# A decode kernel with a gated mix: small loads ahead of w_gate, and the block's end moved ahead of wo's rest

## The chip, the core and the metric

The kernel runs on one core of one Trainium2 chip. Its metric is device microseconds of one execution, as the median of the runs shown; smaller is better. All times below are microseconds unless marked otherwise. Engines are named as in the profile: PE (TensorE matmuls), PEld (its weight loads), DVE (VectorE), ACT (ScalarE), POOL (GpSimd) and SP (SyncE, which issues every load and store of this kernel).

## What is computed

One token of a decoder. Attention with 32 query heads over 8 key/value heads, a cache of 32768 positions and a head size of 128, mixed by a gate with a SwiGLU feed-forward layer. All inputs are bf16.

```python
x = A_x                                        # 1 x 1 x 512
g = sigmoid((x * gate_w).sum(-1, keepdims=True))
q = x @ wq                                     # 512 -> 32 heads x 128
p = softmax(q @ k_cache^T * 128 ** -0.5)       # per head, 4 heads share one of 8 k/v heads
a = (p @ v_cache) as one row of 4096, @ wo     # 4096 -> 512
b = (silu(x @ w_gate) * (x @ w_up)) @ w_down   # 512 -> 1792 -> 512
out = g * a + (1 - g) * b                      # 1 x 1 x 512
```

The caches hold 8 x 32768 x 128 values each, 67 MB for k and 67 MB for v; with the weights 148 MB are read and 1 KB is written.

## The kernel before, in words

The kernel is written engine by engine inside one block (`nc.Block("main")`, L212). Each engine has its own instruction list, and all order between engines is by semaphores written out by hand. Where the block ends, all five engines meet in a barrier: each drains and counts up a semaphore, POOL collects the counts and releases the others. The profile books these instructions on L212.

**SP** (L221 to L271) issues every transfer in one order. First wq (L248), x (L249), the gate's weights (L250), w_gate and w_up (L252, both counting up `sem_f`). Then, for each of the 8 k/v heads g, two halves of k of 4 MB each (`load_k`, L227) and v of 8 MB (`load_v`, L238; the last head's v in two halves, L244). A k load waits until PE has transposed what stood in its page, a v load until PE has used the v before it; the first v load waits until PE is done with w_gate and w_up, whose page it takes over. Behind the last v come w_down (L259) and wo in five pieces of 16, 8, 4, 2 and 2 rows of each partition (L265, `WO_CUTS`), each with a semaphore of its own. Then SP waits for the result row (`sem_dve_row`), stores it (L267) and waits for the store to land.

**PE.** `emit_start` (L385) makes the identity matrix, transposes x, computes q, the gate's sum and the feed-forward layer's first half, and then loops over the 8 heads: `emit_k` twice (transposes of k at L279, copied out by DVE at L646, and scores at L291), `emit_max`, `emit_v` (L332) and `emit_reduce` (L353). `emit_end` (L479) is what comes behind the loop: w_down's 14 strips, the head outputs brought into place, and wo piece by piece. Pieces 0 and 1 (24 rows) go through `emit_strip` (L364), four accumulating strips of 512; ACT copies these strips to SBUF (L543, counting up `sem_part`). Pieces 2 to 4 (8 rows) go through `emit_rows` (L375), four matmuls of 128 columns each; behind piece 2 four more such matmuls add ACT's copy. In the instruction list `emit_end` stands ahead of `emit_start`: a loop of two turns runs `emit_start` in the first turn and `emit_end` in the second.

**ACT** loops over the heads (exponentials, L530; copy of the accumulated outputs, L539), then waits for the last reduction and for PE's strips and makes the copy at L543. **DVE** ends with the transposed outputs (L696), the column vector `O2` (L698) and, when PE has summed everything, the result row (L700). **POOL** sets constants and passes on one semaphore.

Of the kernel before, what the change touches and what calls it, by code (L numbers as in the profile page):

```python
# [5 lines left out]
ACT = mybir.ActivationFunctionType  # L6
ALU = mybir.AluOpType
AX = mybir.AxisListType
BF16 = mybir.dt.bfloat16
# [3 lines left out]
def bass_gated_mix__gqa_block_cached__swiglu_ffn__decode_kernel(  # L13
# [14 lines left out]
    G = A_k_cache.shape[1]  # L28
# [23 lines left out]
    STEP = 16  # L52
    WOJ = H * DH // 128
# [3 lines left out]
    WO_CUTS = [0, 16, 24, 28, 30, 32]  # L57
    WO_ROWS = 24
    OC = NOUT // 128
# [3 lines left out]
    NSTRIP = 4  # L63
# [11 lines left out]
    with ExitStack() as es:  # L75
        def S_(name):
            return es.enter_context(nc.semaphore(name))
# [5 lines left out]
        sem_wo = [S_(f"s_wo{i}") for i in range(len(WO_CUTS) - 1)]  # L83
# [37 lines left out]
        sem_red = S_("s_red")  # L121
# [5 lines left out]
        sem_pe_part = S_("s_pe_part")  # L127
        sem_part = S_("s_part")
        sem_pe_sum = S_("s_pe_sum")
        sem_dve_row = S_("s_dve_row")  # L130
        sem_out = S_("s_out")

        def T(name, shape, dt):
            return es.enter_context(nc.sbuf_tensor(name, shape, dt))
# [11 lines left out]
        sel4 = T("sel4", [128, 16], FP32)  # L146
# [5 lines left out]
        tT = T("tT", [128, FC], BF16)  # L152
        wd = T("wd", [128, FC, NOUT], BF16)
# [15 lines left out]
        O2a = T("O2a", [128, WOJ], BF16)  # L169
        O2 = T("O2", [128, WOJ], BF16)  # L170
        res_row = T("res_row", [128, 128], BF16)

        def P(name, shape, dt):
            return es.enter_context(nc.psum_tensor(name, shape, dt))
# [15 lines left out]
        ps_c = ps_sc[0][:, :]  # L190
        ps_s = ps_sc[1][:, 0:HPG]
        ps_d = ps_sc[1][:, 0:128]
# [11 lines left out]
        part = acc[:, :, :].rearrange("p q d -> p (q d)")  # L204
# [4 lines left out]
        wo_v = page[:, PG_X, 0 : WOJ * NOUT].rearrange("p (j n) -> p j n", j=WOJ)  # L209
        qall = qblk[:, :].rearrange("p (g e c) -> p g e c", e=2, c=2 * HPG)  # L210

        with nc.Block("main") as block:  # L212
            @block.gpsimd
            def _(pool):
                pool.memset(ones_f[:, :], 1.0).then_inc(sem_ones, 1)
                pool.memset(ones_bf[:, :], 1.0).then_inc(sem_ones, 1)
                for g in range(G - 1):
                    pool.wait_ge(sem_v[0], 16 * (g + 1))
                    pool.sem_inc(sem_v[1], 16)

            @block.sync  # L221
            def _(sp):
                def load_k(g, b):
                    if g:
                        sp.wait_ge(sem_fill, UPG * (g - 1) + UPP * (b + 1))
                    src = A_k_cache[0, g, :, :].rearrange("(p b r) d -> p b r d", b=NB, r=R)
                    sp.dma_start(  # L227
                        page[:, PG_K[b], :].rearrange("p (r d) -> p r d", d=DH), src[:, b, :, :]
                    ).then_inc(sem_k[b], 16)

                def load_v(g):
                    if g:
                        sp.wait_ge(sem_v_free, STEP * g)
                    else:
                        sp.wait_ge(sem_pe_h, 1)
                    src = A_v_cache[0, g, :, :].rearrange("(p b r) d -> p b r d", b=NB, r=R)
                    if g < G - 1:
                        sp.dma_start(  # L238
                            vpage.rearrange("p b r d -> p (b r d)"),
                            src.rearrange("p b r d -> p (b r d)"),  # L240
                        ).then_inc(sem_v[0], 16)
                    else:
                        for b in range(NB):
                            sp.dma_start(vpage[:, b, :, :], src[:, b, :, :]).then_inc(  # L244
                                sem_v[b], 16
                            )

                sp.dma_start(wq_v, A_wq.rearrange("(p c) n -> p c n", c=KC)).then_inc(sem_q, 16)  # L248
                sp.dma_start(x_row[0:1, :], A_x[0, :, :]).then_inc(sem_ld_x, 16)  # L249
                sp.dma_start(gw_row[0:1, :], gate_w.unsqueeze(0)).then_inc(sem_ld_g, 16)  # L250
                for w, src in enumerate((B_w_gate, B_w_up)):
                    sp.dma_start(  # L252
                        wgu[:, w, :, :], src.rearrange("(p c) f -> p c f", c=KC)
                    ).then_inc(sem_f, 16)
                for g in range(G):
                    for b in range(NB):
                        load_k(g, b)
                    load_v(g)
                sp.dma_start(  # L259
                    wd[:, :, :], B_w_down.rearrange("(p j) n -> p j n", j=FC)  # L260
                ).then_inc(sem_ld_wd, 16)
                src = A_wo.rearrange("(p j) n -> p j n", j=WOJ)
                for k, s in enumerate(sem_wo):
                    a, b = WO_CUTS[k], WO_CUTS[k + 1]
                    sp.dma_start(wo_v[:, a:b, :], src[:, a:b, :]).then_inc(s, 16)  # L265
                sp.wait_ge(sem_dve_row, 1)
                sp.dma_start(  # L267
                    out[0, 0, :].rearrange("(c n) -> c n", c=OC),
                    res_row[0 : 32 * (OC - 1) + 1 : 32, :],
                ).then_inc(sem_out, 16)  # L270
                sp.wait_ge(sem_out, 16)  # L271

            @block.tensor
            def _(pe):
# [67 lines left out]
                def emit_reduce(i):  # L342
# [15 lines left out]
                            stop=(q == RQ - 1),  # L358
                        )
                    ins.then_inc(sem_red, STEP)  # L360

                def emit_strip(w, vec, j, start, stop):
                    c = j % NSTRIP
                    return pe.matmul(  # L364
                        ps_c[32 * c : 32 * c + 1, :],
                        vec[:, j : j + 1],
                        w[:, j, :],
                        start=start,
                        stop=stop,
                        skip_group_check=True,  # L370
                    )

                def emit_rows(lhsT, rhs, start, stop):
                    for oc in range(OC):
                        ins = pe.matmul(  # L375
                            ps_d[32 * oc : 32 * oc + 1, :],
                            lhsT,
                            rhs[:, oc * 128 : (oc + 1) * 128],
                            start=start,
                            stop=stop,  # L380
                            skip_group_check=True,
                        )
                    return ins

                def emit_start():  # L385
                    pe.wait_ge(sem_dve_r, 1)
# [92 lines left out]
                def emit_end():  # L479
                    pe.wait_ge(sem_dve_tT, 1)  # L480
                    pe.wait_ge(sem_ld_wd, 16)
                    for j in range(FC):
                        emit_strip(wd, tT, j, j < NSTRIP, False)

                    pe.wait_ge(sem_dve_oT2, 1)
                    pe.matmul(
                        ps_m[:, M_O0 : M_O0 + WOJ], pmat[:, :], O2a[:, :], start=True, stop=True
                    ).then_inc(sem_pe_O2, 1)
                    pe.wait_ge(sem_dve_O2, 1)
                    for k, s in enumerate(sem_wo):  # L490
                        pe.wait_ge(s, 16)
                        for j in range(WO_CUTS[k], WO_CUTS[k + 1]):
                            if j < WO_ROWS:
                                ins = emit_strip(wo_v, O2, j, False, j >= WO_ROWS - NSTRIP)
                            else:
                                ins = emit_rows(
                                    O2[:, j : j + 1], wo_v[:, j, :], j == WO_ROWS, j == WOJ - 1
                                )
                        if WO_CUTS[k + 1] == WO_ROWS:
                            ins.then_inc(sem_pe_part, 1)  # L500
                        if WO_CUTS[k] == WO_ROWS:
                            pe.wait_ge(sem_part, 1)
                            emit_rows(sel4[:, 0:1], part, False, False)
                    ins.then_inc(sem_pe_sum, 1)

                with pe.Fori(0, 2, 1) as turn:
                    with pe.If(turn > 0):
# [5 lines left out]
            def _(act):  # L513
# [7 lines left out]
                with act.Fori(0, G * STEP, STEP) as i:  # L521
# [15 lines left out]
                            ).then_inc(sem_exp, 2)  # L537
                    act.wait_ge(sem_v_free, i + STEP)
                    act.activation(part, ps_o[:, :], ACT.Copy).then_inc(sem_acc, STEP)  # L539

                act.wait_ge(sem_red, G * STEP)
                act.wait_ge(sem_pe_part, 1)
                act.activation(part, ps_c, ACT.Copy).then_inc(sem_part, 1)  # L543

            @block.vector
            def _(dve):
# [8 lines left out]
                n = 1  # L555
# [140 lines left out]
                dve.transpose(O2a[:, :], oTs[:, :]).then_inc(sem_dve_oT2, 1)  # L696
                dve.wait_ge(sem_pe_O2, 1)
                dve.tensor_copy(O2[:, :], ps_m[:, M_O0 : M_O0 + WOJ]).then_inc(sem_dve_O2, 1)  # L698
                dve.wait_ge(sem_pe_sum, 1)
                dve.tensor_copy(res_row[:, :], ps_d).then_inc(sem_dve_row, 1)  # L700


# [26 lines left out]
```

## Time and profile before

| what | value |
|---|---|
| median of 3 runs (lowest, highest) | 352.4 (352.34, 352.53) |
| the profiled execution's own time | 352.43 |
| its span, first to last instruction | 350.6 |
| DVE busy | 192.1 (55%) |
| PE busy | 257.8 (74%) |
| ACT busy | 43.0 (12%) |
| read from HBM | 148.11 MB, 422 GB/s over the span |

The profile is taken from one execution. Its span goes from the core's first instruction to its last; 1.8 us of the execution's own time lie outside. An engine's busy time is the union of its instructions. Waiting, branching and issuing instructions are not counted as busy and are marked with a q behind the engine's name (SPq). A wait is put down to what ended last before it. The chain of waits goes back from the last instruction to what released it, step by step. For every transfer the trace also holds the semaphore's increments, one from each DMA engine that has finished its share; times of "increments" below are from there.

### The profile page before, as it was taken

Reading aid. Unit: us, or ns where it says so; the run is one execution under the profiler, and the core shown is the slowest. Engines: PE = TensorE matmul, PEld = TensorE weight load, DVE = VectorE, ACT = ScalarE, POOL = GpSimd, SP = SyncE. Lnnn points to the kernel's source line nnn. Section 1 sums busy time; section 2 is a strip of 40 time slices with the busy share of each in tenths; the row PEclk is TensorE's granted clock in tenths of the full one; section 3 lists DMA queues with packets and bytes.
Section 4 is the critical chain, followed back from the end, with each engine's and each line's share of the span. In section 5 each row is a group of like instructions: output and inputs, shape, how many; then the busy total and the mean of one; then the engine's idle time right before and its main releaser. Section 6 shows DMA issues by size and latency. Waiting matters only on the chain.

```text
span 350.6 us, 8661 instructions
## 1 busy us (share of the span) xinstructions
PE 257.8 (74%) x3871; PEld 211.9 (60%) x3871; DVE 192.1 (55%) x242; ACT 43.0 (12%) x156; POOL 0.4 (0%) x6
## 2 busy tenths in 40 slices
PE   1443987688848994798767993898567993999474
PEld 1113986288816984388626992498527991598431
DVE  4243887068812985088703893098605782298501
ACT  1000000500050002300050003100140004000230
POOL 0000000000000000000000000000000000000000
PEclk9996798599957998799968996799969896899769
DMA  8999998999989999999999998999999999999994
GB/s 329 413 453 419 477 450 377 421 426 456 471 381 419 478 411 422 422 464 464 396 411 422 460 471 381 419 456 434 426 419 426 501 396 411 422 437 441 410 422 193
DMA packets 4914, 148.21 MB, mean 423 GB/s; under 512 B 554, under 2 KB 556, under 8 KB 940
## 3 DMA queue, kind: packets, MB, share of 16 engines
q1 hardware_dynamic: 4908, 148.12, 98.4%
q8 instruction: 5, 0.08, 0.1%
q14 instruction: 1, 0.01, 0.0%
HBM read 148.11 MB, written 0.00 MB: 422 GB/s over the span
## 4 chain that ended last, share of the span: by engine, by line
DMA 61%; PE 30%; DVE 4%; ACT 2%; SPq 1%; issue 1%; ACTq 0%; DVEq 0%
DMA page<-in_A_k_cache_dram 49%; PE pst L279 20%; DMA page<-in_A_wo_dram 12%; PE ps_sc L291 5%; DVE ktT L646 4%; PE ps_o L332 3%; ACT ET L530 1%; ACT L523 1%; SPq L265 0%; DVE pmaxf L651 0%; PE ps_m L317 0%; PE ps_m L353 0%; SPq L252 0%; PE ps_m L313 0%; SPq L244 0%
## 5 line engine op out<-in xcount | busy, mean ns | idle before, releaser
L646 DVE COPY ktT<-pst 128x2048 bf16<-128x2048 bf16 x128 | 155.5, 1224 | 30.2 <-PE pst L279 22.6
L279 PE MATMUL pst<-ident_f,page 128*128 128x128 f32 x1024 | 141.3, 287 | 14.0 <-DMA page<-in_A_k_cache_dram 8.6
L279 PEld LDWEIGHTS pst<-ident_f,page 128*128 128x128 f32 x1024 | 117.5, 147 | 17.6 <-DMA page<-in_A_k_cache_dram 9.1
L291 PE MATMUL ps_sc<-qcur,ktT 128*128 128x8 bf16 x2048 | 67.8, 166 | 8.5 <-DVE ktT L646 8.5
L291 PEld LDWEIGHTS ps_sc<-qcur,ktT 128*128 128x128 bf16 x2048 | 66.7, 97 | 11.1 <-DVE ktT L646 9.9
L332 PE MATMUL ps_o<-page,ET 128*16 128x512 bf16 x512 | 44.8, 528 | 27.1 <-ACT ET L530 27.1
L332 PEld LDWEIGHTS ps_o<-page,ET 128*16 128x16 bf16 x512 | 16.4, 116 | 52.2 <-issue 41.2
L523 ACT ACT_TABLE_LOAD x8 | 10.3, 1283 | 238.7 <-PE ps_m L317 238.7
L669 DVE TENSOR_TENSOR esum<-esum 128x4 f32<-128x4 f32 x8 | 1.3, 163 | 43.3 <-ACT ET L530 43.3
L530 ACT ACTIVATE ET<-ps_sc,nbias 128x128 bf16<-128x128 f32 x64 | 24.0, 559 | 0.7
L673 DVE RECIPROCAL rS<-ps_sc 128x4 f32<-128x4 f32 x8 | 1.5, 183 | 35.5 <-PE ps_sc L344 35.5
L530 ACT ACTIVATION_READ_ACCUMULATOR ET<-ps_sc,nbias 128x1 f32 x64 | 18.5, 288 | 0.0
L651 DVE TENSOR_REDUCE pmaxf<-ps_sc 128x4 f32<-128x512 f32 x16 | 11.1, 692 | 10.4 <-PE ps_sc L291 10.4
L353 PE MATMUL ps_m<-sel,acc 128*128 128x4 f32 x64 | 8.4, 255 | 3.6 <-ACT acc L539 3.6
L353 PEld LDWEIGHTS ps_m<-sel,acc 128*128 128x128 f32 x64 | 7.7, 191 | 4.3 <-ACT acc L539 4.3
L313 PE MATMUL ps_m<-ident_f,pmax 128*4 128x128 f32 x8 | 2.7, 333 | 9.1 <-DVE pmax L653 9.1
L539 ACT ACTIVATE acc<-ps_o 128x512 f32<-128x512 f32 x8 | 4.8, 597 | 35.7 <-PE ps_o L332 35.7
L317 PE MATMUL ps_m<-diag,ones_f 4*128 4x4 f32 x16 | 4.1, 326 | 6.3 <-DVE diag L665 6.3
L317 PEld LDWEIGHTS ps_m<-diag,ones_f 4*128 4x128 f32 x16 | 3.7, 282 | 8.3 <-issue 8.3
L397 PE MATMUL ps_m<-ones_bf,x_row 1*128 1x1 bf16 x4 | 0.3, 172 | 9.2 <-DMA x_row<-in_A_x_dram 9.2
L313 PEld LDWEIGHTS ps_m<-ident_f,pmax 128*4 128x4 f32 x8 | 0.6, 81 | 9.6 <-issue 9.6
L397 PEld LDWEIGHTS ps_m<-ones_bf,x_row 1*128 1x128 bf16 x4 | 0.2, 114 | 9.4 <-DMA x_row<-in_A_x_dram 9.4
(68 smaller groups left out, 54.5 us busy)
## 6 DMA issues: line engine op xcount, KB each, us to landing
page<-in_A_k_cache_dram SPq DMA_DIRECT2D x16, 4096.0 KB, 27.2
page<-in_A_v_cache_dram SPq DMA_DIRECT2D x2, 4096.0 KB, 25.8
page<-in_A_wq_dram SPq DMA_DIRECT2D x1, 4096.0 KB, 12.2
page<-in_A_wo_dram SPq DMA_DIRECT2D x1, 2048.0 KB, 38.7
page<-in_B_w_gate_dram SPq DMA_DIRECT2D x1, 1792.0 KB, 15.4
page<-in_B_w_up_dram SPq DMA_DIRECT2D x1, 1792.0 KB, 19.3
wd<-in_B_w_down_dram SPq DMA_DIRECT2D x1, 1792.0 KB, 34.3
page<-in_A_wo_dram SPq DMA_DIRECT2D x1, 1024.0 KB, 40.8
```

Of the source, the lines that this page charges most:

```text
L279: ins = pe.transpose(pst[u % NST][:, k * 128 : (k + 1) * 128], kv[:, n * 128 : (n + 1) * 128], ident_f[:, :],)
L291: ins = pe.matmul(ps_sc[b][:, col : col + 2 * HPG], kt[:, k, e, :], qcur[:, e, :], start=(e == 0), stop=(e == 1),)
L313: pe.transpose(ps_m[0:HPG, M_A0 : M_A0 + 128], pmax[:, :], ident_f[:, :]).then_inc(sem_t, STEP)
L317: pe.matmul(ps_m[:, M_B0 : M_B0 + HPG], ones_f[0:HPG, :], diag[:, :], start=True, stop=True,).then_inc(sem_b, STEP)
L332: ins = pe.matmul(ps_o[32 * c : 32 * c + RQ * HPG, :], ET[:, n : n + RQ, :].rearrange("p n h -> p (n h)"), vpage[:, b, k * RQ : (k + 1) * ...
L353: ins = pe.matmul(ps_m[:, M_P0 : M_P0 + HPG], acc[:, q, :], sel4[:, q * HPG : (q + 1) * HPG], start=(q == 0), stop=(q == RQ - 1),)
L523: act.activation(nbias[:, :], ps_m[:, M_B0 : M_B0 + HPG], ACT.Copy, scale=-SCALE).then_inc(sem_nbias, STEP)
L530: act.activation(ET[:, b * R : (b + 1) * R, h], sc[:, h, :], ACT.Exp, bias=nbias[:, h : h + 1], scale=SCALE, accum_out=esum[:, b, h : h + ...
L539: act.activation(part, ps_o[:, :], ACT.Copy).then_inc(sem_acc, STEP)
L646: dve.tensor_copy(ktT[:, u % NKT, :], pst[u % NST][:, :].bitcast(BF16)).then_inc(sem_cp, 1)
L651: dve.tensor_reduce(pmaxf[:, b, :], sc, AX.X, ALU.max).then_inc(sem_d, 1)
L673: dve.reciprocal(rS[:, :], ps_s).then_inc(sem_d, 1)
```

## The change

Three things change.

1. SP issues fifteen loads more, between the gate's weights and w_gate. Load n, from 15 down to 1, takes n rows of 256 bytes of wq into n partitions of a new buffer `mark`, which nothing reads. All count up `sem_mark`; POOL waits for the full count of 240 at the end of its part of the block.
2. The block ends earlier. PE's `emit_end` now has only wo's piece 0. Pieces 1 to 4 with their matmuls, ACT's copy of the strips, DVE's copy of the result row, and SP's store with the wait for it, stand behind the block's end, and so behind its barrier. SP has issued all of wo before the barrier. The helpers `emit_strip` and `emit_rows` move out of the block, unchanged but for the engine as an argument; `emit_wo` is new and holds the body of the old loop over the pieces.
3. ACT's wait for the last reduction ahead of its copy of the strips is dropped; the barrier stands there instead.

In PE's instruction list 44 matmuls therefore move from ahead of the loop over the heads to behind the barrier. Nothing else in the loops or in the order of the large transfers changes.

```diff
+        mark = T("mark", [16, 15, 128], BF16)
...
+        def emit_wo(pe, k):
+            pe.wait_ge(sem_wo[k], 16)
+            for j in range(WO_CUTS[k], WO_CUTS[k + 1]):
+                if j < WO_ROWS:
+                    ins = emit_strip(pe, wo_v, O2, j, False, j >= WO_ROWS - NSTRIP)
+                else:
+                    ins = emit_rows(
+                        pe, O2[:, j : j + 1], wo_v[:, j, :], j == WO_ROWS, j == WOJ - 1
+                    )
+            if WO_CUTS[k + 1] == WO_ROWS:
+                ins.then_inc(sem_pe_part, 1)
+            return ins
...
+                pool.wait_ge(sem_mark, 240)
...
                 sp.dma_start(gw_row[0:1, :], gate_w.unsqueeze(0)).then_inc(sem_ld_g, 16)
+                for n in range(15, 0, -1):
+                    sp.dma_start(mark[0:n, n - 1, :], A_wq[0:n, 0:128]).then_inc(sem_mark, 16)
                 for w, src in enumerate((B_w_gate, B_w_up)):
...
-                sp.wait_ge(sem_dve_row, 1)
-                sp.dma_start(
-                    out[0, 0, :].rearrange("(c n) -> c n", c=OC),
-                    res_row[0 : 32 * (OC - 1) + 1 : 32, :],
-                ).then_inc(sem_out, 16)
-                sp.wait_ge(sem_out, 16)
...
-                    for k, s in enumerate(sem_wo):
-                        pe.wait_ge(s, 16)
...
-                    ins.then_inc(sem_pe_sum, 1)
+                    emit_wo(pe, 0)
...
-                act.wait_ge(sem_red, G * STEP)
-                act.wait_ge(sem_pe_part, 1)
-                act.activation(part, ps_c, ACT.Copy).then_inc(sem_part, 1)
...
-                dve.wait_ge(sem_pe_sum, 1)
-                dve.tensor_copy(res_row[:, :], ps_d).then_inc(sem_dve_row, 1)
+
+        pe, act, dve, sp = nc.tensor, nc.scalar, nc.vector, nc.sync
+        for k in range(1, len(sem_wo)):
+            ins = emit_wo(pe, k)
+            if WO_CUTS[k] == WO_ROWS:
+                pe.wait_ge(sem_part, 1)
+                emit_rows(pe, sel4[:, 0:1], part, False, False)
+        ins.then_inc(sem_pe_sum, 1)
+        act.wait_ge(sem_pe_part, 1)
+        act.activation(part, ps_c, ACT.Copy).then_inc(sem_part, 1)
+        dve.wait_ge(sem_pe_sum, 1)
+        dve.tensor_copy(res_row[:, :], ps_d).then_inc(sem_dve_row, 1)
+        sp.wait_ge(sem_dve_row, 1)
+        sp.dma_start(
+            out[0, 0, :].rearrange("(c n) -> c n", c=OC),
+            res_row[0 : 32 * (OC - 1) + 1 : 32, :],
+        ).then_inc(sem_out, 16)
+        sp.wait_ge(sem_out, 16)
```

More of the change, by code (lines that the diff above doesn't have):

```diff
@@ L131, in bass_gated_mix__gqa_block_cached__swiglu_ffn__decode_kernel @@
         sem_out = S_("s_out")
+        sem_mark = S_("s_mark")
         def T(name, shape, dt):
@@ L210, in bass_gated_mix__gqa_block_cached__swiglu_ffn__decode_kernel, with emit_strip, emit_rows @@
         qall = qblk[:, :].rearrange("p (g e c) -> p g e c", e=2, c=2 * HPG)
+        def emit_strip(pe, w, vec, j, start, stop):
+            c = j % NSTRIP
+            return pe.matmul(
+                ps_c[32 * c : 32 * c + 1, :],
+                vec[:, j : j + 1],
+                w[:, j, :],
+                start=start,
+                stop=stop,
+                skip_group_check=True,
+            )
+        def emit_rows(pe, lhsT, rhs, start, stop):
+            for oc in range(OC):
+                ins = pe.matmul(
+                    ps_d[32 * oc : 32 * oc + 1, :],
+                    lhsT,
+                    rhs[:, oc * 128 : (oc + 1) * 128],
+                    start=start,
+                    stop=stop,
+                    skip_group_check=True,
+                )
+            return ins
[7 more added lines that the diff above has]
+                        pe, O2[:, j : j + 1], wo_v[:, j, :], j == WO_ROWS, j == WOJ - 1
+                    )
+            if WO_CUTS[k + 1] == WO_ROWS:
+                ins.then_inc(sem_pe_part, 1)
+            return ins
         with nc.Block("main") as block:
@@ L360, in emit_reduce @@
                     ins.then_inc(sem_red, STEP)
[L362 to L383, printed above, removed]
                 def emit_start():
@@ L482, in emit_end @@
                     for j in range(FC):
-                        emit_strip(wd, tT, j, j < NSTRIP, False)
+                        emit_strip(pe, wd, tT, j, j < NSTRIP, False)
                     pe.wait_ge(sem_dve_oT2, 1)
@@ L489, in emit_end @@
                     pe.wait_ge(sem_dve_O2, 1)
-                    for k, s in enumerate(sem_wo):
-                        pe.wait_ge(s, 16)
[L492 to L503, printed above, removed]
-                    ins.then_inc(sem_pe_sum, 1)
+                    emit_wo(pe, 0)
                 with pe.Fori(0, 2, 1) as turn:
```

## The prediction

> **What bounds the kernel now.** I read the page's time slices first, then the busy times by window, then the chain of waits, then the timeline of the last eight microseconds. The slices show the 16 DMA engines busy from the first slice to the one before last:
>
> ```profile
> DMA  8999998999989999999999998999999999999994
> ```
>
> The windows view (columns: window, length, busy time of PE, PEld, DVE, ACT, POOL, granted PE clock, DMA share, GB/s) says how full:
>
> ```profile
> 40.00:342.00 302.00, 236.15 (x3624) 198.39 (x3622) 174.46 (x204) 40.40 (x152) 0.00 (x0) 0.86 1.00 431
> 342.00:348.00 6.00, 3.79 (x77) 1.28 (x80) 0.76 (x4) 0.60 (x1) 0.00 (x0) 1.00 0.70 277
> 348.00:350.70 2.70, 0.24 (x8) 0.06 (x8) 0.29 (x1) 0.00 (x0) 0.00 (x0) 0.73 0.00 0
> ```
>
> For 302 us the DMA share is 1.00 at 431 GB/s, so compute waits for bytes and its length does not matter there. The time can change in three places only: a gap in the DMA stream, the moment the last weight piece lands, and what follows that landing. The chain of waits (start, length, what) shows the last two:
>
> ```profile
> 306.01 41.90 DMA page<-in_A_wo_dram
> 347.91 0.04 issue
> 347.96 0.31 PE ps_sc L375 x8
> ...
> 348.29 0.29 DVE res_row L700
> ```
>
> Here wo's last piece lands at 347.91; eight matmuls and a copy follow, then the store. The records of L212, the block's end, close the run (op, durations, first and last start):
>
> ```profile
> L212 SPq COMPARE_BRANCH  x1: 33/33/33, 350.3 to 350.3; - x1
> L212 SPq DRAIN  x1: 7/7/7, 350.4 to 350.4; - x1
> ...
> L212 PEldq EVENT_SEMAPHORE  x1: 51/51/51, 350.6 to 350.6; - x1
> ```
>
> SP sees the store landed at 350.27 (the branch's start in the trace), drains, GpSimd collects and releases, and PE's release ends the span at 350.64. The profiled execution took 352.43, so 1.79 lie outside the span; the median of the runs shown is 352.40, 0.03 below it.
>
> **Part 1: the block's end leaves the end.** Behind the store SP now has one wait and nothing else. Removed from the end: 350.64 - 350.27 = 0.37; the wait itself takes about 0.03 (the branch's 33 ns). Term: **-0.34**.
>
> The barrier reappears between wo's first piece and its second. What covers it is PE's wait there:
>
> ```profile
> 343.50 1.03 PE L364 MATMUL ps_sc<-page,O 128*1 128x512 bf16 x16 [0.28 <-DVE O L698]
> ...
> 345.39 0.10 PEld L364 LDWEIGHTS ps_sc<-page,O 128*1 128x1 bf16 x8 [1.36 <-DMA page<-in_A_wo_dram]
> ```
>
> (Timeline: start, length, then in brackets the idle time before and what ended it.) At the old end PE's branch, loop step, branch and drain took from 347.97 to 348.47, 0.50, and the barrier from GpSimd's collecting (350.46) to PE's release (350.64) 0.18. From the last of the sixteen weight loads, 345.39 - 1.36 = 344.03, or the last matmul's end, 344.53, to which the drain may hold: PE is free at 344.7 to 345.2. The second piece lands at 345.34. So nothing is late, with 0.1 to 0.6 to spare. If that cover were gone, what is late next is the ACT copy of the strips (0.60, done at 346.70, needed at 346.88) and then the fourth and fifth pieces (347.31 and 347.96): some 0.5 more of delay is swallowed. Queued behind PE's barrier are only its own 44 matmuls. ACT has left its loop at 341, DVE at 343.5, SP has issued wo by 308.7, and GpSimd's new wait for 240 was met long before. Term: **0**, and anything up to about 0.5 late still costs 0. ACT's dropped wait for the reduction is covered by the barrier.
>
> **Part 2: the fifteen loads on SP.** They are queued ahead of w_gate. The nearest rows (start, length):
>
> ```profile
> 1.18 0.32 SPq L249 DMA_DIRECT2D x_row<-in_A_x_dram  x1
> 1.55 0.23 SPq L250 DMA_DIRECT2D gw_row<-in_gate_w_dram  x1
> 1.82 0.36 SPq L252 DMA_DIRECT2D page<-in_B_w_gate_dram  x1
> ```
>
> One issue costs 0.23 to 0.43 (the latter is wo's usual issue) plus 0.05 between: 15 x 0.28 to 0.48 = 4.2 to 7.2. w_gate is issued at 6.0 to 9.0 in place of 1.82, and its first packet follows about 1.0 later (wq: issue 0.74, first packet 1.75), at 7 to 10. wq keeps every engine busy until its first engine is done at 12.48 (its sixteen semaphore increments run from 12.48 to 12.96). So 2.5 to 5.5 are to spare and no gap opens; w_up and the first two k loads follow at 0.5 each. The next, v's first load, was issued at 24.80 with the queue full until 40. Term: **0** while SP is not held up; the rival below is that it is.
>
> **Part 3: the fifteen loads on the DMA engines.** x_row (one row) had one landing from an engine, the store (four rows) four, so a load of n rows makes n data packets and n semaphore packets: 120 pairs. The store's data packets took 15 ns, semaphore packets 9, so a pair is 24 ns. Evenly spread that is 7.5 pairs, 0.18 per engine; all fifteen loads on one engine make 0.36 there. Whether it costs anything depends on whose engine it is. wo's last piece has its sixteen increments at 345.91 to 346.37 (ten engines), 347.16, and 347.59, .67, .74, .82, .91. The five late engines are those that each fetched a 16 KB block of PE's program:
>
> ```profile
> q8 instruction: 5, 0.08, 0.1%
> ```
>
> (k's first load still had its sixteen within 0.48 of each other but for one, 1.4 behind the rest after the first fetch at 23.4; by 80 us five were 1.7 to 2.0 behind the first, and they stay so to the end.) A pair on one of the ten is free, on the last five it is paid. Bounds of the term: 0 and +0.36; below nothing is excluded, since every engine already runs full. A harder price: x_row and gw_row landed 0.18 apart, 12.86 and 13.04, and 15 x 0.18 = 2.7 is the upper end if each load holds its engine so long. Against it: w_gate's sixteen increments follow wq's by 4.28 to 4.32 each in order, so two such loads moved no engine by more than about 0.04. I take the packets' price, and the even share: **+0.18**.
>
> The Trainium skill, page "DMA: Bandwidth & Descriptors", section "Why a DMA increments its semaphore by 16 and not by 1", says that a load of n rows runs on the n lowest-numbered engines. The one and four landings above agree with the number of engines; no run here shows which they are. By it the lowest engine takes all fifteen pairs, and the term would be +0.36 if that engine is also the last one.
>
> **Part 4: the program's layout.** 44 matmuls (88 instructions of load and multiply) move from ahead of PE's loop to behind it. The fifth block was fetched at 69.63, late in the loop's first pass, with some 11 matmuls of L332 and ten of the reduction still ahead. Moved on by 88 instructions, it would not come until the tail; the engine it held back, the last one, would then be on time and the end 347.82 in place of 347.91. I take half of that: **-0.05**.
>
> **Sum.** 350.64 - 0.34 + 0.18 - 0.05 = 350.43 for the span. With 1.79 around it 352.22. Outside the span four engines are now done two to five microseconds before SP; how much of the 1.79 that frees, no row shows. Bounds: 0 and about 0.5 (the spread with which engines entered, SP at 0.00, PE at 0.32, is the nearest row); I take 0.1. **Forecast 352.1**, 0.3 below the median. What a measurement of this kernel can tell from no change is about 0.2%, 0.7 us: 351.7 to 353.1 counts as the same.
>
> **Rivals.**
> - *More is hidden than the span shows* (faster). Nothing is paid for the packets, the fifth fetch leaves (-0.09) and 0.3 or more of the 1.79 is overlapped: 352.4 - 0.34 - 0.09 - 0.3 = 351.67 and down to 351.4. For it: ten of sixteen engines have 1.2 to 2.0 to spare. Against: nothing shows the 1.79 from inside. Chance **0.17**.
> - *SP's queue fills* (slower). One row shows that an issue can be held:
>
> ```profile
> L265 SPq DMA_DIRECT2D page<-in_A_wo_dram x5: 432/432/2688, 304.1 to 306.0; - x5
> ```
>
> The last wo piece took 2.69 where its neighbours took 0.43, as the ninth transfer under way. If eight transfers is the limit, the marks stop at about 4 us, with wq, x, gw and five marks under way, and move on only as wq drains: some three to seven marks are left at 12.5, 0.3 each, then w_gate with 0.36 + 0.65: the engines stand idle for 1.5 to 2.7. 352.1 + 1.5 to 2.7 = 353.6 to 354.8. It decides as soon as w_gate's issue passes 11.5. Against: the release at 308.7 came with no transfer's landing (the oldest landed at 312 to 314), which fits a count of descriptors, nine per engine and transfer, better; then the limit was near 72 to 80 per engine, and after this change the fullest has at most 79 less the four or more that wq has consumed. Chance **0.13**.
> - *A small load costs more than its packets.* Between 0.36 and 2.7 on one engine; on a late one all of it, on an early one all beyond 1.5 to 2.0: 352.6 to 354.4. Chance **0.08**, half of it above 353.1.
> - *PE's tail is not in its instruction memory* (slower). A 16 KB packet of code took 1.02 to 1.08, to which waiting behind a 32 KB packet (about 2.0 at the start) may come: 1 to 3 late, less the 0.6 to 1.1 of cover in part 1, so 352.6 to 354.3. It decides when PE's second wo piece starts later than 345.9. Against: the tail's last instruction lies where the old block's end lay, 0 or 1 instructions off, PE jumped there and back with no fetch after 70 us, and no fetch left a gap on PE. Chance **0.04**.
>
> The Trainium skill, page "Runtime: NRT & Kernel Launch", section "Instruction fetch mechanics", says that a taken branch whose target is outside the current two-page window waits for a fetch. Here PE branched back over its whole loop at 342.06 without one, so the trace does not bear it out for this loop; by it this rival would be the likely one.
>
> **How the numbers follow.** The forecast has **0.58** and its own range is 351.7 to 352.7. The range of 351.4 to 353.6 leaves out most of the full queue (0.12) and the far ends of the others (0.06). Faster by over 0.2%: 0.17. Within: 0.58 + 0.04 = 0.62. Slower: 0.13 + 0.04 + 0.04 = 0.21.
>
> **What would show it.** Right: the records of the block's end at about 345 and none behind the store; PE's second wo piece at its landing; w_gate issued at 6 to 9 and wq's increments followed by w_gate's with no gap; wo's last increments spread by a further 0.2 to 0.4. Wrong: mark issues of over 0.5 us, w_gate's landing later than 17.6, a fetch of code between 342 and 347, or a last landing beyond 348.3.

## The result and the profile after

The changed kernel takes **354.31 us** (median of 3 runs, 354.23 to 354.36) where the kernel before takes 352.40: a ratio of 1.0054, 95% interval 1.0040 to 1.0067. It is slower by 1.9. The forecast was 352.1, with a range of 351.4 to 353.6.

The profiled execution took 354.31, its span is 352.99. Three differences make up the whole:

| stretch | before | after | difference |
|---|---|---|---|
| start to the landing of wo's last piece | 347.91 | 350.61 | +2.70 |
| that landing to the end of the span | 2.73 | 2.38 | -0.35 |
| time outside the span | 1.79 | 1.32 | -0.47 |
| the execution's own time | 352.43 | 354.31 | +1.88 |

So the end and the time outside the span became shorter, by 0.82 together where 0.44 was forecast, and the stream of transfers became longer by much more. The chain of waits of the kernel after shows the late landing:

```profile
308.20 42.40 DMA page<-in_A_wo_dram
350.61 0.04 issue
350.65 0.31 PE ps_sc L227 x8
...
350.99 0.29 DVE res_row L704
```

The same steps stand behind the landing as before, 2.70 later. Where the stream lost them is in the windows view (window, length, busy times of PE, PEld, DVE, ACT and POOL, granted PE clock, DMA share, GB/s). The kernel before:

```profile
0.00:12.50 12.50, 1.22 (x4) 0.92 (x4) 4.07 (x16) 1.28 (x1) 0.45 (x6) 1.00 0.87 351
12.50:17.50 5.00, 4.30 (x38) 1.66 (x38) 1.81 (x4) 0.00 (x0) 0.00 (x0) 1.00 0.99 424
17.50:23.00 5.50, 2.06 (x33) 1.03 (x37) 3.14 (x7) 0.17 (x1) 0.00 (x0) 1.00 1.02 438
```

The kernel after:

```profile
0.00:12.50 12.50, 1.22 (x4) 0.92 (x4) 4.07 (x16) 1.28 (x1) 0.44 (x6) 1.00 0.84 338
12.50:17.50 5.00, 4.02 (x38) 1.46 (x38) 1.95 (x4) 0.17 (x1) 0.00 (x0) 1.00 0.74 297
17.50:23.00 5.50, 0.57 (x16) 0.50 (x16) 3.01 (x7) 0.00 (x0) 0.00 (x0) 0.73 1.04 447
```

For five microseconds behind wq, where the run of small loads is worked off, the DMA share is 0.74 in place of 0.99 and 297 GB/s are moved in place of 424. Before and behind that the two are nearly alike (351 and 338, 438 and 447). The rate is lost while work is queued: w_gate was issued long before, as SP's timeline of the kernel after shows:

```profile
1.55 0.23 SPq L289 DMA_DIRECT2D gw_row<-in_gate_w_dram  x1
1.82 5.48 SPq L291 DMA_DIRECT2D mark<-in_A_wq_dram  x15
7.34 0.36 SPq L293 DMA_DIRECT2D page<-in_B_w_gate_dram  x1
```

The fifteen issues took 5.5 in all and w_gate's came at 7.34, five before wq ran out. The semaphore increments tell how the loss is spread. Before, w_gate's sixteen lie at 16.78 to 17.26. After, they are a staircase: 17.49, .56, .57, .96, .97, 18.07, .17, .41, .52, 19.48, .81, .94, 20.02, .09, .41, 21.07. A later transfer keeps such a lag, since every engine's queue stays full: wo's last piece has its increments at 346.63 to 350.61, over 3.98, where before they spread over 2.00. The last engine ends the run.

At the end the forecast picture holds. The records of the block's end (L250, formerly L212; op, durations, first and last start) and of SP's last wait in the kernel after:

```profile
L250 POOLq EVENT_SEMAPHORE  x2: 17/17/17, 346.8 to 346.8; - x2
...
L250 PEldq DRAIN  x1: 465/465/465, 346.3 to 346.3; - x1
...
L250 PEldq EVENT_SEMAPHORE  x1: 51/51/51, 346.9 to 346.9; - x1
```

```profile
L710 SPq EVENT_SEMAPHORE  x1: 17/17/17, 353.0 to 353.0; - x1
```

And PE's work on wo's pieces, from the timeline of the kernel after:

```profile
345.66 1.03 PE L216 MATMUL ps_sc<-page,O 128*1 128x512 bf16 x16 [0.30 <-DVE O L692]
348.05 0.60 PE L216 MATMUL ps_sc<-page,O 128*1 128x512 bf16 x8 [1.35 <-DMA page<-in_A_wo_dram]
```

PE was through the barrier at 346.95 and then waited for the second piece, which landed at 348.00. The barrier cost nothing there, and no code was missing behind it. In that kernel the second piece was itself late; in the kernel with the moved block alone (below) PE was through at 344.15 and the piece landed at 345.23.

### The profile page after: what moved, and what is told of

Same layout as the page of the kernel before. It is cut to its first block, busy times and chain, and to the rows that moved or that the text cites. A ratio compares the mean times of both kernels' runs of the same rounds, so it can differ in the third digit from the quotient of the medians.

```text
span 353.0 us, 8676 instructions
## 1 busy us (share of the span) xinstructions
PE 257.9 (73%) x3871; PEld 211.9 (60%) x3871; DVE 192.2 (54%) x242; ACT 43.0 (12%) x156; POOL 0.4 (0%) x6
## 4 chain that ended last, share of the span: by engine, by line
DMA 52%; PE 35%; DVE 6%; ACT 3%; SPq 3%; issue 1%; ACTq 0%; DVEq 0%
DMA page<-in_A_k_cache_dram 40%; PE pst L314 22%; DMA page<-in_A_wo_dram 12%; PE ps_sc L326 6%; PE ps_o L367 5%; DVE ktT L640 5%; SPq L291 1%; ACT ET L528 1%; ACT L521 1%; PE ps_m L388 1%; DVE pmaxf L645 1%; SPq L306 0%; PE ps_m L352 0%; ACT acc L537 0%; PE ps_m L348 0%
## 5 line engine op out<-in xcount | busy, mean ns | idle before, releaser
L462 PE MATMUL pst<-page,xT 128*1 128x448 bf16 x32 | 3.2, 573 | 5.4 <-DMA page<-in_B_w_up_dram 5.4
## 6 DMA issues: line engine op xcount, KB each, us to landing
page<-in_B_w_up_dram SPq DMA_DIRECT2D x1, 1792.0 KB, 17.6
```

## The experiments

**Theory A**, formed from the staircase: a small load in a run of small loads costs each DMA engine that takes part far more than its two packets, about 0.24 us; the engine with all fifteen is some 3.6 late, and the end of the run goes by the last engine. **Rivals**: the moved code and the barrier (B); w_gate's late issue (B2); what the loads share, such as the places they read (H) or the semaphore they count up (S); the uneven distribution alone (E); the number of rows in flight (C). Every kernel below was timed beside runs of the kernel before on the same chip, and each ratio is to those.

**The two halves of the change, each alone.** The first kernel is the one before with the loads; the second is the one after without them.

```diff
 # e1_marks_only: the kernel before, with these lines and mark's buffer and semaphore
+                for n in range(15, 0, -1):
+                    sp.dma_start(mark[0:n, n - 1, :], A_wq[0:n, 0:128]).then_inc(sem_mark, 16)
...
+                pool.wait_ge(sem_mark, 240)
 # e2_block_only: the change without these lines
```

> The kernel before with the fifteen small loads, block's end unmoved. Theory A (in a run of small loads each one costs its engines about 0.24 us, so the engine with all fifteen is 3.6 us late at w_gate and the last landing follows it): w_gate's increments spread over 3 to 4 us, wo's last increment at 350.4 to 350.8, span 353.2 to 353.5, time 354.9 to 355.2. Rival B (the loss comes from the moved code and the barrier in the middle): no loss here, wo's last increment at 347.9 to 348.3, time 352.4 to 352.8.

> The change without the fifteen loads. Theory A: wo's last increment within 0.2 us of 347.9, nothing behind the store but one wait, span 350.2 to 350.4; time 351.5 to 351.7 if the part of the time outside the span falls from 1.8 to 1.3 us with the block's move, 352.0 to 352.2 if it does not. Rival B: the loss is here, last increment at 350 or later, time 354.

Measured: the loads alone 355.13, ratio 1.0078 (1.0062 to 1.0093), that is +2.65. The moved block alone 351.62, ratio 0.9978 (0.9969 to 0.9987), that is -0.86. The two add up to +1.8, the change's +1.9. Rival B falls. The window behind wq, in the loads alone and in the moved block alone:

```profile
12.50:17.50 5.00, 4.16 (x38) 1.53 (x38) 1.67 (x4) 0.00 (x0) 0.00 (x0) 1.00 0.74 294
```

```profile
12.50:17.50 5.00, 4.12 (x38) 1.46 (x38) 2.13 (x4) 0.17 (x1) 0.00 (x0) 1.00 0.99 421
```

The gap comes with the loads and goes with them. wo's last increment was at 350.27 (theory A had expected 350.4 or later) and 347.81. The moved block alone is the fastest kernel of this study and beats both kernels.

**The loads apart from each other** (e3). One behind each of the first fifteen k and v loads:

```diff
+                def put_mark(n):
+                    if n > 0:
+                        sp.dma_start(mark[0:n, n - 1, :], A_wq[0:n, 0:128]).then_inc(sem_mark, 16)
                 for g in range(G):
                     for b in range(NB):
                         load_k(g, b)
+                        put_mark(15 - 3 * g - b)
                     load_v(g)
+                    put_mark(13 - 3 * g)
```

> The change with the fifteen loads issued one behind each of the first fifteen k and v loads. Theory A1 (the 0.24 us is paid for a run of small descriptors that come faster than the engine can be supplied, not for a load as such): the increments of a k load between spread as without the loads, wo's last increment at 347.8 to 348.3, time 351.5 to 352.2. Theory A2 (each load costs its engine 0.24 us wherever it stands): last increment at 350 to 351, time 354 to 354.6.

Measured: 351.96, ratio 0.9988 (0.9979 to 0.9997); wo's last increment at 348.25, 0.44 behind that of the moved block alone, the first 0.33 behind. The same fifteen loads cost 0.34 in time here and 2.7 in a run. A1's numbers came and A2 falls: it is the run that costs. Whether it costs because the engine can't be supplied fast enough, as A1 has it, no run shows. What is left, 0.33 to 0.44, is of the size of fifteen times the 24 ns of packets of the prediction's part 3, but that may be chance: the first increment is held by nearly as much as the last.

**Another place** (e6). The run behind the first head's two k loads, so that w_gate is issued at 1.8:

> The change with the run of fifteen loads behind the first head's two k loads in place of ahead of w_gate, so that w_gate is issued at 1.8 again. Theory A (the run costs the same wherever it stands): w_gate's increments as without the loads, the spread of 3 to 4 us first in the first v load, wo's last increment at 349.5 to 351, time 353.3 to 354.6. Rival B2 (w_gate's late issue at 7.3 is what hurts): no spread anywhere, time 351.6 to 352.2.

Measured: 354.23, ratio 1.0051 (1.0034 to 1.0067). w_gate's increments are those of the kernel before (16.73 to 17.31); the first v load's lie at 60.50 to 64.23. The gap has moved with the run, to where it is worked off:

```profile
35.00:40.00 5.00, 5.00 (x63) 4.89 (x62) 4.46 (x4) 0.00 (x0) 0.00 (x0) 0.84 0.99 419
40.00:45.00 5.00, 5.00 (x107) 4.88 (x105) 4.65 (x5) 0.00 (x0) 0.00 (x0) 1.00 0.94 367
45.00:50.00 5.00, 3.66 (x55) 3.40 (x55) 3.43 (x4) 0.00 (x0) 0.00 (x0) 1.00 0.99 423
```

The moved block alone, without the loads, in the second of these windows:

```profile
40.00:45.00 5.00, 5.00 (x107) 4.88 (x105) 4.64 (x5) 0.00 (x0) 0.00 (x0) 1.00 1.11 478
```

B2 falls. The loss shows more in the GB/s than in the share here, since a packet of the v load that meets the run is stretched and counts as busy meanwhile (up to 3.58, where it takes 2.42).

**How many loads, on how many engines.** Fifteen loads of one row, fifteen of 16 rows, and five of 16 rows:

```diff
-                    sp.dma_start(mark[0:n, n - 1, :], A_wq[0:n, 0:128]).then_inc(sem_mark, 16)
+                    sp.dma_start(mark[0:1, n - 1, :], A_wq[0:1, 0:128]).then_inc(sem_mark, 16)  # e4
+                    sp.dma_start(mark[:, n - 1, :], A_wq[0:16, 0:128]).then_inc(sem_mark, 16)  # e5; e10: n from 5
```

> The change with fifteen loads of one row each in place of 15 down to 1 rows. Theory A, with the one row always on the same engine: fifteen of w_gate's increments as without the loads (16.8 to 17.3), one 3 to 4 us later, wo's last increment at 349.5 to 351, time 353 to 354.5. Rival C (the staircase comes from the number of rows in flight, 120 in all, not from the loads per engine): all w_gate increments within 1 us, wo's last at 348 to 348.5, time 351.6 to 352.2.

> The change with fifteen loads of 16 rows each, so that every DMA engine has one row of every load. Theory A (about 0.24 us for each small load of a run, on each engine that takes part): no staircase, all sixteen of w_gate's increments 3.4 to 4.3 us later than without the loads, at 20.3 to 21.5; the code fetches come on top, wo's last increment at 351.0 to 352.0, time 354.8 to 355.8. Rival E (the loss is only that some engines have more loads than others): the increments at 17 to 18, time 351.6 to 352.6.

> The change with five loads of 16 rows in place of the fifteen. With fifteen of them w_gate's increments were 2.2 to 3.0 us later than without. Theory A, price per load: a third of it, 0.7 to 1.0 us on all engines, wo's last increment at 348.5 to 348.9, time 352.2 to 352.6. Theory A5 (the first few loads of a run are free, as x and the gate's weights seem to be): 0.3 us or less, time 351.6 to 351.9.

Measured, with w_gate's lag as the mean of its sixteen increments against wq's, less the 4.30 of the kernel before:

| kernel | w_gate's lag | first and last increment | wo's last | time, ratio (interval) |
|---|---|---|---|---|
| the change (7.5 loads per engine on average) | 1.86 | 17.49, 21.07 | 350.61 | 354.31, 1.0054 (1.0040 to 1.0067) |
| fifteen of one row | 0.12 | 16.75, 19.08 | 348.20 | 352.07, 0.9988 (0.9978 to 0.9997) |
| fifteen of 16 rows | 2.67 | 18.96, 20.30 | 350.60 | 354.41, 1.0060 (1.0043 to 1.0077) |
| five of 16 rows | 0.91 | 17.22, 18.50 | 349.08 | 352.90, 1.0013 (1.0003 to 1.0023) |

With one row a single engine is late, by about 2.0 (19.08, the others 16.75 to 17.17): 0.13 a load. A is right that the load's own engine pays, but its size was too high for this case. Rival C has the landing and the time that it named, 348.20 and 352.07, but not its increments, which were to lie within 1: one engine is late with fifteen rows in flight. The end is well under A's 349.5: it fits an early engine, one that no code fetch had held, 2.1 late (346.1 + 2.1 = 348.2).

With 16 rows the staircase is gone and all engines are late: 2.67 / 15 = 0.18 a load; five loads give 0.91 / 5 = 0.18 again, so A5's free start is not there. With 0.24 a load, A had expected more of the fifteen loads of 16 rows (increments at 20.3 to 21.5, 354.8 to 355.8) and missed all of it. The five loads ended 0.2 to 0.3 above what A expected. Rival E falls: with fifteen loads on every engine alike the time is that of the staircase, which has 7.5 on average.

In the change itself the price is 1.86 / 7.5 = 0.25 on average, more than either. On the engine with all fifteen loads it is (21.07 - 17.03) / 15 = 0.27, with 17.03 the mean before. So one price for all cases does not exist, and 0.13 to 0.27 a load is all that these runs give. The window of the fifteen loads of 16 rows shows the loss at its largest:

```profile
12.50:17.50 5.00, 4.39 (x38) 1.66 (x38) 1.95 (x4) 0.01 (x1) 0.00 (x0) 1.00 0.63 253
```

**What in a load costs.** One load with 225 pieces of 256 bytes; each load from rows and columns of its own; a semaphore for each load; rows of 2 KB:

```diff
+                sp.dma_start(                                                        # e7
+                    mark[0:15, :, :],
+                    A_wq[0:15, 0:3840].rearrange("p (n w) -> p n w", w=256)[:, :, 0:128],
+                ).then_inc(sem_mark, 16)
...
+                        mark[0:n, n - 1, :], A_wq[16 * n : 17 * n, 128 * n : 128 * (n + 1)]   # e8
...
+                    sp.dma_start(mark[0:n, n - 1, :], A_wq[0:n, 0:128]).then_inc(sem_mark[n], 16)  # e9
...
+                    sp.dma_start(big[0:n, n - 1, :], A_wq[0:n, 0:1024]).then_inc(sem_mark, 16)  # e12
```

> The change with one load of 15 rows of 15 separate pieces of 256 bytes: 225 pieces, more than the 120 of the change, but one semaphore count per engine in place of up to fifteen. Theory A3 (the price is per load, with its semaphore): w_gate's increments less than 0.6 us later than without, time 351.6 to 352.3. Theory A4 (the price is per short piece): fifteen engines 2 to 4 us late, wo's last increment at 349.8 to 351.6, time 353.4 to 355.3.

Measured: 352.38, ratio 0.9996 (0.9987 to 1.0006). w_gate's increments at 17.59 to 18.15 are 0.8 to 0.9 late on all engines, wo's last at 348.75. That is between the two expectations and nearer to A3: with fifteen pieces of one load the engines are some 0.83 late, with fifteen loads of one piece 2.63 (both against the kernel before). It is no clean price of a piece, though. The load has fifteen rows and shows fifteen increments, yet all sixteen of w_gate's are late: the engine that took no part was held as well, so engines do hold each other up. The window stays full, but at 389 GB/s:

```profile
12.50:17.50 5.00, 3.73 (x36) 1.16 (x36) 1.44 (x3) 0.00 (x0) 0.00 (x0) 1.00 1.01 389
```

> The change with each of the fifteen loads reading rows and columns of wq of its own; in the change all fifteen read the same 256 bytes of row 0, fourteen those of row 1, and so on. Theory H (fifteen engines or loads reading the same few places of HBM wait for each other): w_gate's increments within 1 us, time 351.6 to 352.4. Theory A without H: the same staircase as the change, spread of 3 to 4 us, time 353.9 to 354.6.

Measured: 354.05, ratio 1.0047 (1.0030 to 1.0064), increments from 17.61 to 20.80. The staircase is there; H falls.

> The change with a semaphore of its own for each of the fifteen loads (GpSimd waits for all fifteen). Theory A (each load's count holds its own DMA engine, 0.13 us with one engine at work and about 0.24 with all, whichever semaphore it goes to): as the change, w_gate's increments over 3 to 4 us, time 353.9 to 354.6. Theory S (engines wait for each other at one shared semaphore, which makes 0.24 out of 0.13): spread near 2 us, wo's last increment at 348 to 349.5, time 351.8 to 353.2.

Measured: 354.27, ratio 1.0056 (1.0038 to 1.0074), increments from 17.52 to 21.20, wo's last at 350.57. S falls.

> The change with rows of 2048 bytes in place of 256, into a page that v fills later; v's first load waits for them, long before its turn. Theory A (a fixed price per load, which covers the bytes while those take less than it): the same staircase, wo's last increment at 350.3 to 351.0, time 354.0 to 354.7. Theory A6 (the price comes on top of the bytes): 15 times 0.07 more on the worst engine, last increment at 351.3 to 352, time 355 to 355.8. Theory W (the price is one of short rows): no staircase, 351.6 to 353.2.

Measured: 354.95, ratio 1.0068 (1.0050 to 1.0086), wo's last at 351.48. W falls: short rows are not the cause. Between A and A6 it does not decide: the time lies between, the landing where A6 put it, but not for A6's reason. w_gate's first increment was already at 19.70, 2.9 late, so all engines were slowed and not the worst one most; the 2 KB packets took 199 ns on average, where wo's take 84 to 96.

**The time outside the span** (e11). The moved block without the loads, and all engines wait for the store at their end:

```diff
-        sp.wait_ge(sem_out, 16)
+        for eng in (sp, nc.gpsimd, pe, act, dve):
+            eng.wait_ge(sem_out, 16)
```

> The block's move without the fifteen loads, and all five engines wait at their end for the store's landing (no barrier). Every kernel with the moved block had 1.3 us outside its span, both with the block's end at the end 1.8. Theory O (what lies behind the last instruction on four engines is done while SP still waits for the store): here nothing can be done early, outside 1.7 to 1.9, span 350.2 to 350.4, time 352.0 to 352.2. Rival (the 0.5 us belongs to the barrier's own instructions at the end): outside 1.3, time 351.5 to 351.8.

Measured: 352.14, ratio 0.9991 (0.9981 to 1.0001); the profiled execution 352.08 with a span of 350.27, so 1.81 outside, where the moved block alone had 351.59 and 350.27, 1.32 outside. Theory O holds: with equal spans, 0.5 is gained when four engines may finish ahead of SP.

## Why the prediction was wrong

**Where it failed** is part 3, the price of the loads on the DMA engines: +0.18 was taken, +2.70 was measured at wo's last landing. Two signs that the prediction had named for this case came: w_gate's landing beyond 17.6 (21.07) and a last landing beyond 348.3 (350.61). The step took the packets' 15 and 9 ns as the time that a load holds an engine. In the profile of the kernel after the 256-byte packets do take 15 to 18 ns, but while the run is worked off the engines' share is 0.74, so they stand idle between packets. In the kernel with fifteen one-row loads (e4) the semaphore's increments come at 13.11, 13.29, 13.46, 13.63, 13.81 and so on to 15.59, 0.174 to 0.183 apart, while their data packets had all started between 12.36 and 12.85. Data leaves quickly, the loads complete one by one.

The step had this spacing in hand, the 0.18 between the landings of x and the gate's weights. It set it aside because those two loads had moved none of w_gate's increments; what two loads on one engine hide said nothing of fifteen. Its upper end, 15 x 0.18 = 2.7, equals the measured +2.70 by luck. With one engine at work the lag is 2.0 and not 2.7, and in the change the engine with all fifteen loads was 4.0 late at w_gate (21.07 against a mean of 17.03). How 4.0 becomes 2.70 at the end is an inference, since the trace does not number the engines: an early engine that is 4.0 late ends near 346.13 + 4.04 = 350.17, and one of wo's increments is at 350.19; the three behind it, 350.49 to 350.61, fit engines with fewer loads that a code fetch had held as well.

That each completion is what holds the engine is what e7 (one completion, a smaller loss) and e3 (completions beside large packets, little loss) point to; it was not isolated: loads without a semaphore of any kind were not tried.

The rival that named it, "a small load costs more than its packets", had 0.08 and 352.6 to 354.4. The time fell into its range; the 4.0 on one engine lies beyond its 2.7.

**Part 3, whose engine pays.** The prediction counted on the ten early engines to swallow up to 1.2 to 2.0. That holds: fifteen one-row loads cost their engine 2.0 and the run only 0.4 at the landing. With 15 down to 1 rows the worst engine's 4.0 was beyond any slack. The Trainium skill ("DMA: Bandwidth & Descriptors", "Why a DMA increments its semaphore by 16 and not by 1") has a load of n rows, up to 16, run on the n lowest-numbered engines; one late engine in e4, sixteen late ones in e5 and the staircase of the change agree with always the same ones, though no run shows their numbers.

**Part 1, the block's end** was right: -0.34 forecast, -0.35 measured from the landing to the end (-0.27 in the moved block alone), and the barrier hidden ahead of wo's second piece, with 1.0 to spare in the kernel after (346.95 against 348.00) and 1.1 in the moved block alone, where 0.1 to 0.6 was forecast.

**Outside the span** the term was mis-sized: 0.1 taken, bounds 0 to 0.5, measured 0.47 here, and 0.5 between e2 and e11. The moved block alone is therefore worth 0.86, more than what was called measurable.

**Part 2, SP's queue** was right: issues of 0.25 to 0.44, w_gate at 7.34 within the 6 to 9 given, no gap from it. The rival of a full queue did not occur.

**Part 4, the layout** had the wrong mechanism. The fifth code fetch did not move to the tail in any run: it came at 73.0 in e2 and at 153.4 in the kernel after, and e2 still has six late increments at wo's last piece (347.06 to 347.81). Nor does the layout alone set its place: the kernel after and the runs e2 to e10 and e12, which change nothing in PE's program, have it anywhere from 72.9 to 265.9. wo's last landing in e2 is 0.10 earlier than before, where 0.05 was taken; that is one execution of each and not for the reason given. PE's tail ran without a gap, so the rival of the missing code did not occur.

What stays open: what a completion waits for, why a load costs 0.13 with one engine at work, 0.18 with all alike and 0.25 in the staircase, and whether the place written matters: all these loads write the first partitions of SBUF, and no run wrote others.

## What to carry to other kernels

In a kernel bound by its transfers, don't issue small loads back to back into the queue of the large ones: here each cost every engine it used 0.13 to 0.27 us, five to eleven times its packets' 24 ns, and one engine's lag lasts to the end. Put them between large transfers (0.34 in all for fifteen here), or merge them into one load (0.6 to 0.8 here, for more pieces). Look at a transfer's sixteen increments and not only at its landing: the last engine sets the time, and lags on the others, up to its own, are free. Work that closes the kernel, such as a barrier of all engines, belongs ahead of the last wait for data, so that only the storing engine is left at the end.

## What the runs showed of the hardware that was not expected

- A run of small loads completes one load at a time on an engine, 0.174 to 0.183 apart with fifteen one-row loads, though most of its data packets start 20 ns apart.
- Engines that finish ahead of the last one shorten the time outside the span by 0.5 (1.32 against 1.81 with equal spans).
- Each 16 KB block of code holds the one DMA engine that fetches it back by about 1.5 for the rest of the run (increments of the first k load, behind one fetch: fifteen at 30.80 to 31.28, one at 32.65; at wo's last piece, behind five, ten lie at 345.91 to 346.37 and five at 347.59 to 347.91). The place of the fifth fetch varied between kernels with the same or nearly the same PE program: 69.6 to 76.2 in nine of them, and 109.6, 153.4, 190.5, 227.7 and 265.9 in the others, mostly 37 to 38 apart, about one pass of the loop over the heads.
